# A fused attention and two-layer feed-forward kernel: where x is split, and in what order the second layer takes its blocks

## The chip, the cores and the metric

The kernel runs on one core of a Trainium2 chip. The metric is the time of one execution on the device in microseconds (us). The engines are called PE (TensorE: matmuls and transposes; its weight loads are the row PEld), DVE (VectorE), ACT (ScalarE), POOL (GpSimd) and SP (SyncE, which issues all DMAs here). Each runs its own instructions strictly in the order in which the program lists them.

## The reference

Two batches of 12 heads of softmax attention with a tanh cap, then a feed-forward layer with a softmax-weighted unit and a layer norm, then a gated feed-forward layer.

```python
scores = cap * np.tanh(scale * np.matmul(q, k.transpose(0, 1, 3, 2)) / cap)
attn = softmax(scores);  x = (attn @ v) as 896 tokens x 768          # float32
h = x @ w_in                                                          # 768 -> 1024
solu = h * softmax(h)
ln = (solu - mean(solu)) / np.sqrt(var(solu) + 1e-06) * g_ln
y = ln @ w_out                                                        # 1024 -> 768
out = (sigmoid(y @ w_gate) * (y @ w_val)) @ moe2_w_out                # 768 -> 1536 -> 768
```

The weights arrive as 64-bit floats, so the kernel receives two 32-bit words for each.

## The kernel before, in words

**Precision.** Each operand of the four big products is split in a high part (`hi`, float32 rounded to the matmul's format) and the rest (`lo`). A product is three matmuls: hi by hi, hi by lo, lo by hi (`prod`, `l1_mms`). So each weight tile and each activation tile needs a cast on ACT for hi and a subtract on DVE or POOL for lo.

**Weights.** A chunk is 128 x 512 of a weight. `chunk_steps` turns the two words of a 64-bit float into float32 and splits it, in six steps: first step (drop the sign; L349 on DVE, or L347 on ACT where `act` is set), clamp (L352), shift (L353), sign and exponent (L354), low word (L355, followed by `upper`: the scale by `g_ln`, L334, and the hi cast on ACT, L336), and the lo subtract (L339). `chunk_stream` puts the steps of many chunks into the queue `todo`, two chunks overlapping, with each chunk's DMA three chunks ahead. `fill(k)` takes the next k steps out of the queue at the place where it is called. The twelve chunks of the second layer's weight come through `w2_stream`, two for each of six output blocks; their split tiles are called `w_hl`.

**First layer and norm.** The 896 tokens go in seven tiles t of 128. `x_split(t)` makes xh (ACT, L391) and xl (L392) from x, in two buffers each. `l1_mms(t)` are 36 matmuls of 512 columns (L405) into PSUM. Then `ln_max` (DVE, L415), `ln_exp` (ACT, L420), `ln_he` (DVE, L423), `ln_stats` (DVE, L429 to L434, and a power on POOL, L435), `ln_norm` (one small DVE instruction, L439, then the pass over the tile, on ACT in L441 for tiles 2 to 6), `ln_trans` (8 transposes on PE, L449) and `ln_evac` (ACT L455 writes lnhi, DVE L456 writes lnlo). The tile `e` that L420 writes, and that the transposes read at the end, has one buffer. Tiles 0 and 1 run beside the attention. For t from 2 to 6 the loop near L590 writes out the order by hand: half of the 36 matmuls, a step of `todo`, the other half, the transposes of tile t-1, and then the norm of tile t with `fill` calls and the split for tile t+2 between its parts.

**Second layer.** `l2(m, g)` is 24 matmuls for output block m (of six) and token group g: group 0 is tiles 0 to 2 (384 columns), group 1 is tiles 3 to 6 (512 columns). It reads both `w_hl` tiles of block m, asks for four more steps of `todo` behind it, and leaves the evacuation (`y_hi` on ACT, L649, `y_lo` on DVE, L650) to run behind the next block. Its PSUM pool has two buffers.

**Order.** Until the end of the second layer PE, ACT, DVE and POOL keep the order in which the code is written (`tc.manual_schedule`). The third and fourth layers come after that; their weight chunks have the first step on ACT already.

Of the kernel before, what the change touches and what calls it, by code (L numbers as in the profile page):

```python
# [32 lines left out]
K3 = DM // P  # L33
# [109 lines left out]
def network(ctx: ExitStack, tc: tile.TileContext, sh, general, w_in, w_mid, w_gv, w_fin, outT):  # L143
    nc = tc.nc
# [159 lines left out]
    def fill(k):  # L304
        for _ in range(min(k, len(todo))):
            todo.popleft()()
# [51 lines left out]
            steps += [upper]  # L358
        return steps + [lower]

    def chunk_stream(chunks):

        raw = {}

        def load(c):
            if c < len(chunks):
                raw[c] = chunk_load(chunks[c][0])

        order = []
        for c, (src, dst, scale) in enumerate(chunks):  # L370
            steps = chunk_steps(lambda c=c: raw[c], dst, scale)
            last = steps[-1]
            steps[-1] = lambda last=last, c=c: (last(), load(c + AHEAD))
            n = len(steps)
            order += [(n // 2 * c + k + 2 * (k == n - 1), c, step) for k, step in enumerate(steps)]
        for c in range(AHEAD):
            load(c)
        todo.extend(step for _, _, step in sorted(order, key=lambda x: x[:2]))
# [34 lines left out]
    def ln_max(t):  # L413
        sts[t] = lin2.tile([P, 24], F32, tag="st", name="st")
        nc.vector.tensor_reduce(sts[t][:, 0:1], hts[t].rearrange("p a b -> p (a b)"), AX.X, ALU.max, negate=True)  # L415

    def ln_exp(t):
        st = sts[t]
        lnes[t] = lin2.tile([P, F1], F32, tag="e", name="e", bufs=1)
        nc.scalar.activation(lnes[t], hts[t].rearrange("p a b -> p (a b)"), AF.Exp, bias=st[:, 0:1], accum_out=st[:, 1:2])  # L420
# [93 lines left out]
    def w2_stream():  # L514
        chunk_stream([
            (w_mid[m].rearrange("p a b -> p (a b)")[:, c * CH:(c + 1) * CH], w2_dst(m, c), sh.g_sb[:, c * 4:c * 4 + 4])
            for m in range(K3) for c in range(2)
        ])

    NS = 2 * NPAIR  # L520
    for s in range(-1, NS):
        m = s + 1
# [45 lines left out]
    t = L1_BESIDE  # L568
# [18 lines left out]
    for t in range(L1_BESIDE, 7):  # L587
        if t == 3:
            x0.close()
        if t == 2:  # L590
            lnt2 = lns.enter_context(tc.tile_pool(name="lnt2" + sfx, bufs=1, side="right", reuse_waits="tile"))
            ln_hi[1] = lnt2.tile([P, K2, NT - G1], F32R, name="lnhi1")
            ln_lo[1] = lnt2.tile([P, K2, NT - G1], F32R, name="lnlo1")
            w2p = lns.enter_context(tc.tile_pool(name="w2p" + sfx, bufs=W2_BUFS, side="right", reuse_waits="tile"))
        k = FILL_T if wide else 0
        if t > L1_BESIDE:
            mms = l1_mms(t)
            run(mms[:18])
        fill(k)
        run(mms[18:])  # L600
        if t > L1_BESIDE:
            ln_trans(t - 1)
        else:
            run(late[:1])
        ln_max(t)
        ln_exp(t)
        if t == 6:
            ln_he(t)
            ln_stats(t)
            ln_evac(t - 1)  # L610
            ln_norm(t, True)
            fill(3 * k)
            continue
        fill(k)
        ln_he(t)
        ln_stats(t)
        if t > L1_BESIDE:
            ln_evac(t - 1)
        else:
            run(late[1:])  # L620
        if t + 2 < 7:
            x_split(t + 2, nc.gpsimd)
        fill(k)
        ln_norm(t, True)
        fill(k)
    wi.close()
    ytp = ctx.enter_context(tc.tile_pool(name="ytp" + sfx, bufs=1, side="left", reuse_waits="tile"))
    y_hi = ytp.tile([P, K3, NT], F32R, name="y_hi")
# [27 lines left out]
    l2(1, 0)  # L656
    ln_trans(6)
    ln_evac(6)
    l2(2, 0)
    for m in range(3):  # L660
        l2(m, 1)
    for m in range(3, K3):
        for g in range(2):
            l2(m, g)
    run(y_evac)
# [93 lines left out]
```

## Time and profile before

| what | value |
|---|---|
| time, median of 3 runs (lowest to highest) | 514.54 us (514.01 to 514.84) |
| time of the profiled execution | 515.4 us |
| span of its trace, first to last instruction | 513.5 us |
| PE busy over the span | 495.0 us |
| mean granted PE clock (1.0 is 2.4 GHz) | 0.993 |
| tiles 2 to 6 of the first layer and their norm | 131 to 180 us of the span |
| second layer | 180 to 251 us |
| third layer | 251 to 422 us |
| fourth layer and end | 422 to 513.5 us |

How to read it: PE is busy nearly always, so the time can fall only where PE stands idle or runs at the lower of its two clock levels, and it rises wherever PE is made to wait. The timeline view lists instructions with their start, length, and in brackets the idle time of the engine before them and what ended it.

### The profile page before, as it was taken

What the parts mean: (1) busy time and instruction counts of PE and PEld (TensorE: products, weight loads), DVE (VectorE), ACT (ScalarE), POOL (GpSimd) and SP (SyncE); (2) the same over time, 40 slices, a digit from 0 to 9 for tenths busy, and PEclk for the clock granted to TensorE, in tenths of its full rate; (3) what the DMA queues carried; (4) which work ended last, traced back from release to release, by engine and by line L of the source; (5) the groups of instructions that cost most, each with busy time, mean ns of one, the idle gap of its engine ahead of it and who ended that gap; (6) DMA issues with size and microseconds to landing.
All of it is one profiled execution on the core that took longest, in us unless ns stands there. A gap on an engine that the chain in (4) does not pass through costs nothing.

```text
span 513.5 us, 6510 instructions
## 1 busy us (share of the span) xinstructions
PE 495.0 (96%) x2480; PEld 386.8 (75%) x2480; DVE 336.4 (66%) x580; ACT 239.2 (47%) x326; POOL 57.1 (11%) x41
## 2 busy tenths in 40 slices
PE   8999999999998977999999999999999999999995
PEld 4333333553776767899899999999999999999995
DVE  1776854174788888569889888887877777551000
ACT  5999999575243432124454444434334433321000
POOL 0010101021212100000002111111111011000000
PEclk9999999999999997999999999999999999999999
DMA  7676665010101113115555444343333443500001
GB/s 253 185 214 178 207 184 157 18 38 19 61 0 41 42 43 122 58 66 165 168 160 171 141 140 123 124 123 92 106 93 122 124 123 101 158 37 37 19 36 41
DMA packets 19058, 55.04 MB, mean 107 GB/s; under 512 B 3212, under 2 KB 6156, under 8 KB 19020
## 3 DMA queue, kind: packets, MB, share of 16 engines
q1 hardware_dynamic: 19020, 54.56, 34.7%
q8 instruction: 21, 0.34, 0.3%
q14 instruction: 17, 0.14, 0.1%
HBM read 51.68 MB, written 2.79 MB: 106 GB/s over the span
## 4 chain that ended last, share of the span: by engine, by line
PE 76%; ACT 14%; DVE 7%; issue 2%; POOL 0%; ACTq 0%; POOLq 0%
PE big L635 34%; PE l4o L635 17%; PE l2o L635 11%; PE big L405 5%; ACT e L198 5%; ACT e L220 5%; PE big L192 3%; PE o L238 3%; DVE e L423 1%; ACT wi_hi L336 1%; DVE lnlo L456 1%; PE big L449 1%; PE sums L246 1%; ACT e L420 1%; PE warm L125 1%
## 5 line engine op out<-in xcount | busy, mean ns | idle before, releaser
L635 PE MATMUL big<-y_hi,w_hl 128*128 128x448 f32 x576 | 161.7, 362 | 0.0
L635 PEld LDWEIGHTS big<-y_hi,w_hl 128*128 128x128 f32 x576 | 107.9, 187 | 7.9
L635 PE MATMUL big<-y_lo,w_hl 128*128 128x448 f32 x288 | 104.6, 363 | 0.0
L336 ACT CAST w_hl<-cvt 128x512 fp32r<-128x512 f32 x66 | 40.8, 618 | 86.0 <-PE big L635 46.4
L635 PE MATMUL l4o<-p_hi,w_hl 128*128 128x448 f32 x288 | 80.7, 361 | 0.0
L355 DVE SCALAR_TENSOR_TENSOR cvt<-w_raw,cvt 128x512 uint32<-128x512 uint32 x78 | 72.8, 934 | 1.2
L635 PE MATMUL l2o<-lnhi,w_hl 128*128 128x384 f32 (+1 forms) x192 | 57.9, 379 | 6.3 <-DVE w_hl L339 6.3
L339 DVE TENSOR_TENSOR w_hl<-cvt,w_hl 128x512 fp32r<-128x512 f32 x66 | 45.3, 686 | 26.1 <-ACT w_hl L336 25.7
L347 ACT ACTIVATE cvt<-w_raw 128x512 f32<-128x512 f32 x54 | 36.2, 671 | 49.5 <-DVE w_hl L339 29.8
L635 PEld LDWEIGHTS l4o<-p_hi,w_hl 128*128 128x128 f32 x288 | 54.0, 187 | 3.9
L635 PEld LDWEIGHTS big<-y_lo,w_hl 128*128 128x128 f32 x288 | 54.1, 188 | 3.1
L354 DVE SCALAR_TENSOR_TENSOR cvt<-w_raw,cvt 128x512 uint32<-128x512 uint32 x78 | 53.6, 687 | 1.4
L708 POOL TENSOR_TENSOR p_lo<-sg,p_hi 128x896 fp32r<-128x896 f32 x12 | 30.5, 2538 | 210.7 <-ACT p_hi L707 210.7
L198 ACT ACTIVATE e<-big,cap_inv 112x896 f32<-112x896 f32 x48 | 46.6, 1038 | 14.8 <-PE big L192 14.8
L635 PE MATMUL l4o<-p_lo,w_hl 128*128 128x448 f32 x144 | 52.3, 363 | 0.0
L352 DVE TENSOR_SCALAR cvt<-cvt 128x512 f32<-128x512 f32 x78 | 33.7, 433 | 22.5 <-ACT cvt L347 22.3
L220 ACT ACTIVATE e<-e,cap_abs 112x896 f32<-112x896 f32 x48 | 48.1, 1073 | 0.0
L635 PEld LDWEIGHTS l2o<-lnhi,w_hl 128*128 128x128 f32 x192 | 37.2, 197 | 11.3 <-DVE w_hl L339 7.2
L238 PE MATMUL o<-e,v 112*64 112x448 f32 x192 | 43.4, 552 | 0.4 <-ACT to L254 0.3
L192 PE MATMUL big<-qk_raw 64*112 64x448 f32 x192 | 43.0, 559 | 0.3 <-ACT e L198 0.3
L353 DVE TENSOR_SCALAR cvt<-cvt 128x512 uint32<-128x512 uint32 x78 | 37.0, 476 | 1.6
L635 PE MATMUL l2o<-lnlo,w_hl 128*128 128x384 f32 (+1 forms) x96 | 36.0, 375 | 0.0
(81 smaller groups left out, 497.5 us busy)
## 6 DMA issues: line engine op xcount, KB each, us to landing
w_raw<-in_w_gv SPq DMA_DIRECT2D x36, 512.0 KB, 3.7
w_raw<-in_w_fin SPq DMA_DIRECT2D x18, 512.0 KB, 3.6
w_raw<-in_w_in SPq DMA_DIRECT2D x12, 512.0 KB, 4.2
w_raw<-in_w_mid SPq DMA_DIRECT2D x12, 512.0 KB, 4.9
qk_raw<-in_qk SPq DMA_DIRECT2D x12, 448.0 KB, 4.3
v<-in_v SPq DMA_DIRECT2D x12, 224.0 KB, 4.1
out_t<-ob SPq DMA_DIRECT2D x12, 224.0 KB, 2.3
qk_raw<-rd SPq DMA_DIRECT2D x22, 112.0 KB, 3.0
```

The costliest lines, as they stand in the source:

```text
L192: nc.tensor.matmul(sc[j][:KC, c, :S], r[d, 1, kc * KC:(kc + 1) * KC], r[d, 0], start=True, stop=True)
L198: nc.scalar.activation(e, es[n, u][:KC, :, :S], AF.Tanh, scale=sh.cap_inv[:KC])
L220: nc.scalar.activation(es[n, u], es[n, u], AF.Exp, scale=sh.cap_abs[:KC])
L238: nc.tensor.matmul(o[d, :S], vs[i][:, kc, d], e[j][:, c], start=(kc == 0), stop=(kc == 3))
L336: nc.scalar.copy(st["hi"], w)
L339: v.tensor_tensor(st["lo"], st["w"], f32(st["hi"]), ALU.subtract)
L347: first = lambda t, lo, hi: nc.scalar.activation(f32(t), f32(hi), AF.Abs)
L352: word(lambda t, lo, hi: v.tensor_scalar(f32(t), f32(t), as_f32(W_MOST), as_f32(W_LEAST), ALU.min, ALU.max)),
L353: word(lambda t, lo, hi: v.tensor_scalar(t, t, 3, REST, ALU.logical_shift_left, ALU.bitwise_and)),
L354: word(lambda t, lo, hi: v.scalar_tensor_tensor(t, hi, TOP, t, ALU.bitwise_and, ALU.bitwise_or)),
L355: word(lambda t, lo, hi: (v.scalar_tensor_tensor(t, lo, 29, t, ALU.logical_shift_right, ALU.bitwise_or), upper())),
L635: nc.tensor.matmul(out, l, r[kx], start=(first and m == 0), stop=(last and m == 2))
```

## The change

It does four things. In the norm loop `x_split(t + 2)` moves from behind the statistics to a place between `ln_max` and `ln_exp`, and its subtract goes from POOL to DVE. The `fill(k)` that stood between the statistics and `ln_norm` moves behind `ln_norm`. The second layer's chunks get their first step on ACT (`act=True`). And in the second layer `l2(2, 0)` no longer comes before group 1 of blocks 0 and 1; the order is now (0,0), (1,0), (0,1), (1,1), (2,0), (2,1) and so on.

```diff
-    def chunk_stream(chunks):
+    def chunk_stream(chunks, act=False):
...
-            steps = chunk_steps(lambda c=c: raw[c], dst, scale)
+            steps = chunk_steps(lambda c=c: raw[c], dst, scale, act)
...
             for m in range(K3) for c in range(2)
-        ])
+        ], act=True)
...
         ln_max(t)
+        if t + 2 < 7:
+            x_split(t + 2)
         ln_exp(t)
...
             run(late[1:])
-        if t + 2 < 7:
-            x_split(t + 2, nc.gpsimd)
-        fill(k)
         ln_norm(t, True)
-        fill(k)
+        fill(2 * k)
...
-    l2(2, 0)
-    for m in range(3):
+    for m in range(2):
         l2(m, 1)
-    for m in range(3, K3):
+    for m in range(2, K3):
         for g in range(2):
             l2(m, g)
```

The lines behind the change are numbered up to two lower than before (L650 becomes L649, L635 becomes L634).

DVE, end of the norm of tile 2 and start of that of tile 3 (`st` holds a tile's statistics, `cvt` a chunk in conversion):

```order
 L456 TENSOR_TENSOR lnlo_143<-big,lnhi_142 128x8x128
-L353 TENSOR_SCALAR cvt<-cvt 128x512
-L439 TENSOR_SCALAR st<-st 128x1
-L354 SCALAR_TENSOR_TENSOR cvt<-w_raw,cvt 128x512
-L349 TENSOR_SCALAR cvt<-w_raw 128x512
-L415 TENSOR_REDUCE st<-big 128x1
+L439 TENSOR_SCALAR st<-st 128x1
+L353 TENSOR_SCALAR cvt<-cvt 128x512
+L354 SCALAR_TENSOR_TENSOR cvt<-w_raw,cvt 128x512
+L415 TENSOR_REDUCE st<-big 128x1
+L392 TENSOR_TENSOR xl<-x_159,xh 128x768
 L339 TENSOR_TENSOR w_hl<-cvt,w_hl 128x512
```

L439 now follows lnlo directly, the step L349 is gone from DVE, and the subtract L392 stands behind the maximum L415.

ACT at the same place, tiles 2 and 3:

```order
 L336 CAST w_hl<-cvt 128x512
+L391 CAST xh<-x_159 128x768
 L420 ACTIVATE e,st<-big,st 128x1024
 L455 CAST lnhi_142<-big 128x8x128
+L441 ACTIVATE e<-e,st 128x1024
+L347 ACTIVATE cvt<-w_raw 128x512
 L391 CAST xh<-x_159 128x768
-L441 ACTIVATE e<-e,st 128x1024
 L420 ACTIVATE e,st<-big,st 128x1024
```

The cast L391 now stands ahead of the exponential L420 of its tile, and the step L347 behind the norm's last pass L441.

PE, what follows the transposes of tile 6 in the second layer, in the kernel before (`w_hl_1607` is the first weight tile of block 2, `lnhi0` and `lnlo0` are group 0):

```order
L449 MATMUL big_1612<-ident_92,e_1518 128x128 x8
L635 MATMUL l2o_1640<-lnhi0_142,w_hl_1607 128x384
L635 MATMUL l2o_1640<-lnlo0_143,w_hl_1607 128x384
L635 MATMUL l2o_1640<-lnhi0_142,w_hl_1607 128x384 x2
L635 MATMUL l2o_1640<-lnlo0_143,w_hl_1607 128x384
```

And in the changed kernel (`w_hl_1197` is the first weight tile of block 0, `lnhi1` and `lnlo1` are group 1):

```order
L449 MATMUL big_1612<-ident_92,e_1518 128x128 x8
L634 MATMUL l2o_1623<-lnhi1_1190,w_hl_1197 128x512
L634 MATMUL l2o_1623<-lnlo1_1191,w_hl_1197 128x512
L634 MATMUL l2o_1623<-lnhi1_1190,w_hl_1197 128x512 x2
L634 MATMUL l2o_1623<-lnlo1_1191,w_hl_1197 128x512
```

PE now goes on with a block whose weights it has used already, and needs the lnhi and lnlo of tile 6, just transposed, instead of the weights of block 2.

## Rows read from the trace of the kernel before

**Rows 1.** The page: busy time by engine, share of the span, instructions.

```profile
PE 495.0 (96%) x2480; PEld 386.8 (75%) x2480; DVE 336.4 (66%) x580; ACT 239.2 (47%) x326; POOL 57.1 (11%) x41
```

**Rows 2.** Timeline of PE, its six waits: start, length, instruction, [idle before, releaser].

```profile
148.92 1.09 PE L449 MATMUL big<-ident,e 128*128 128x128 f32 x8 [0.83 <-ACT e L441]
160.00 1.09 PE L449 MATMUL big<-ident,e 128*128 128x128 f32 x8 [1.79 <-ACT e L441]
169.78 1.09 PE L449 MATMUL big<-ident,e 128*128 128x128 f32 x8 [0.49 <-ACT e L441]
...
186.71 0.62 PE L635 MATMUL l2o<-lnhi,w_hl 128*128 128x384 f32 x2 [2.13 <-DVE w_hl L339]
...
190.51 0.62 PE L635 MATMUL l2o<-lnhi,w_hl 128*128 128x384 f32 x2 [1.19 <-DVE w_hl L339]
...
196.68 1.01 PE L635 MATMUL l2o<-lnhi,w_hl 128*128 128x384 f32 x2 [2.95 <-DVE w_hl L339]
```

**Rows 3.** Timeline of DVE, the conversion step behind lnlo in tiles 2 to 4.

```profile
145.80 1.67 DVE L353 TENSOR_SCALAR cvt<-cvt 128x512 uint32<-128x512 uint32 x1
...
155.49 1.94 DVE L355 SCALAR_TENSOR_TENSOR cvt<-w_raw,cvt 128x512 uint32<-128x512 uint32 x1
157.46 0.69 DVE L334 TENSOR_TENSOR cvt<-cvt,g_sb 128x512 f32<-128x512 f32 x1
...
166.57 1.75 DVE L349 TENSOR_SCALAR cvt<-w_raw 128x512 uint32<-128x512 uint32 x1
```

**Rows 4.** Timeline of POOL, the subtract of x in tile 3.

```profile
155.04 1.84 POOL L392 TENSOR_TENSOR xl<-x,xh 128x768 fp32r<-128x768 f32 x1
```

**Rows 5.** Timeline of DVE, the same steps where POOL is idle.

```profile
186.58 0.68 DVE L355 SCALAR_TENSOR_TENSOR cvt<-w_raw,cvt 128x512 uint32<-128x512 uint32 x1
...
188.36 0.43 DVE L353 TENSOR_SCALAR cvt<-cvt 128x512 uint32<-128x512 uint32 x1
...
189.43 0.42 DVE L349 TENSOR_SCALAR cvt<-w_raw 128x512 uint32<-128x512 uint32 x1
```

**Rows 6.** Timeline of ACT, the norm of tile 3.

```profile
150.10 1.12 ACT L420 ACTIVATE e<-big,st 128x1024 f32<-128x1024 f32 x1 [1.23 <-PE big L449]
...
152.10 0.84 ACT L391 CAST xh<-x 128x768 fp32r<-128x768 f32 x1
...
158.71 1.24 ACT L441 ACTIVATE e<-e,st 128x1024 f32<-128x1024 f32 x1
```

**Rows 7.** Timeline of DVE, the norm of tile 3.

```profile
151.34 1.22 DVE L423 TENSOR_TENSOR e<-big,e 128x1024 f32<-128x1024 f32 x1 [1.07 <-ACT e L420]
...
154.36 1.22 DVE L456 TENSOR_TENSOR lnlo<-big,lnhi 128x1024 fp32r<-128x1024 f32 x1
...
158.07 0.21 DVE L439 TENSOR_SCALAR st<-st 128x1 f32<-128x1 f32 x1
...
158.99 1.22 DVE L415 TENSOR_REDUCE st<-big 128x1 f32<-128x1024 f32 x1
```

**Rows 8.** Timeline of DVE, the subtract of x where DVE makes it already.

```profile
104.87 0.88 DVE L392 TENSOR_TENSOR xl<-x,xh 128x768 fp32r<-128x768 f32 x1
...
124.59 1.54 DVE L392 TENSOR_TENSOR xl<-x,xh 128x768 fp32r<-128x768 f32 x1 [1.37 <-ACT xh L391]
```

**Rows 9.** The chain that ended last: tile 6's matmuls; start, length, what.

```profile
170.87 8.23 PE big L405 x36
```

**Rows 10.** Timeline of DVE, lnlo of tile 6.

```profile
194.47 1.23 DVE L456 TENSOR_TENSOR lnlo<-big,lnhi 128x1024 fp32r<-128x1024 f32 x1 [0.70 <-ACT lnhi L455]
```

**Rows 11.** Busy time by stretch: PE, PEld, DVE, ACT, POOL (instructions), PE clock, DMA share, GB/s.

```profile
196.10:202.80 6.70, 6.12 (x19) 6.03 (x20) 6.53 (x13) 1.55 (x3) 0.00 (x0) 0.50 0.27 88
...
239.00:252.00 13.00, 13.00 (x66) 11.78 (x65) 11.95 (x23) 6.60 (x12) 0.00 (x0) 1.00 0.51 151
```

**Rows 12.** The page's groups: the first step on ACT; busy us, mean ns | idle before.

```profile
L347 ACT ACTIVATE cvt<-w_raw 128x512 f32<-128x512 f32 x54 | 36.2, 671 | 49.5 <-DVE w_hl L339 29.8
```

**Rows 13.** The waits view: us in total, times, longest.

```profile
ACT cvt L347 <- DMA w_raw<-in_w_gv: 12.0, 10, 2.4
```

## The prediction

> **What bounds the kernel now.** I read the page first: PE is busy 495.0 us of a span of 513.5 us [rows 1], so all that other engines do counts only where PE waits for it. Then the timeline of PE from 131 us on. Behind the attention PE waits six times for more than 0.3 us at places that the change touches [rows 2]. Three waits, of 0.83, 1.79 and 0.49 us, stand before the transposes of tiles 2, 3 and 4 and end with L441, the norm's last pass on ACT. Three more, of 2.13, 1.19 and 2.95 us, stand in the second layer and end with a weight's lo subtract, L339 on DVE. Together 9.4 us. Last the busy time by stretch: from 196.1 to 202.8 us the granted clock is 0.50, the lower level of 1.2 GHz, and PE's 19 matmuls there take 6.12 us [rows 11]; it fell some 2.3 us into the longest of the six waits.
>
> Why L441 comes late is read beside DVE. In tile 3 lnlo (L456) ends at 155.58, and L439, on which L441 waits, starts only at 158.07 [rows 7]: in between stand a conversion step of 1.94 us and L334 [rows 3]. The same three steps take 0.68, 0.43 and 0.42 us where POOL is idle [rows 5] and 1.94, 1.67 and 1.75 us in tiles 2 to 4 [rows 3], each while POOL makes its subtract of x, 155.04 to 156.88 in tile 3 [rows 4].
>
> **The change part by part.** *Subtract and step taken from between the statistics and L439.* L439 now follows L456. From L420's start at 150.10 to L456's end at 155.58 are 5.48 us; with L439 (0.21), L441 (1.24) and the transposes (1.09) [rows 2, 6, 7] this makes 8.0 us, some 8.2 with the handovers. This is a loop, since L420 of the next tile waits for the transposes to free `e` [rows 6]. PE itself needs 8.23 us for a tile's 36 matmuls [rows 9] and about 1 us for its transposes, 9.2 us. So the loop, which was 11.1 us in tile 3 (L420 at 150.10, transposes done at 161.09), falls below PE's own pace with about 1 us to spare, and all three waits go: 0.83 + 1.79 + 0.49 = 3.1 us. What is late next there is PE itself.
>
> *Split of x at the head of the norm.* It puts an ACT cast of 0.84 us [rows 6] ahead of L420 and a DVE subtract ahead of L423. The cast needs its buffer back from the tile's matmuls, so it starts with L415 and lies beside it (1.22 us [rows 7]): free. The subtract took 0.88 us where DVE made it undisturbed and 1.54 us beside a POOL instruction [rows 8]; I take 0.88, since POOL has none here any more. It lies in DVE's wait of 1.07 us for L420 [rows 7], beside one conversion step of some 0.4 us that stood there before; together they need about 1.2 us and have that of L420. So 0 us, at worst 3 x (1.54 - 0.88) = 2.0 us, of which the spare of 1 us per tile takes all. If that cover were gone, it would cost the 0.88 us three times.
>
> *First step on ACT.* Twelve times 0.42 us leave DVE [rows 5] and twelve times 0.67 us come to ACT [rows 12], which is busy 239 of 513 us [rows 1]. Two of them fall into the attention, behind the exponentials, where ACT then waits for PE; four stand in the norm loop behind an L441, and six between the `y_hi` of the second layer. On PE's path only one was seen on DVE, the L349 between the second layer's first wait and its second: its removal shortens the wait of 1.19 us by 0.3 to 0.4 us. I take 0.3. What queues behind an L347 on ACT is a `y_hi`, then DVE's `y_lo`, then the next L339; what holds it is the DMA of its words (a rival below). The Trainium skill's page "ScalarE: Activation LUTs" (section Rules for kernel authors) speaks against this part: simple element-wise work belongs on VectorE. The trace agrees as to the length, 671 ns on ACT [rows 12] against 0.42 us on DVE [rows 5]; if the longer step were on the path, the sum would lose 12 x 0.25 = 3 us, and by ACT's idle half it loses nothing.
>
> *The order of the second layer.* The first wait (2.13 us) stays: it hangs on the norm of tile 6 on DVE, which begins when PE has made that tile and so only moves along. The third wait was for block 2's weights. It ended at 196.68 [rows 2]. Now PE waits for lnlo of tile 6 instead, which ended at 194.47 + 1.23 = 195.70 [rows 10], 1.0 us sooner. Before, two matmuls of block 2 ran ahead of the wait; now one does, of hi by hi, so I count 0.8 us, and some 2.1 us stay idle, in two pieces. Block 2's weights get the 48 matmuls of blocks 0 and 1 in group 1 as cover, by 8.23 us for 36 of the same width [rows 9] some 11 us, and were 1 us later than lnlo.
>
> *The clock.* If it stays up, the 6.12 us of matmuls at the lower level [rows 11] take half: 3.0 us. Bounds: 0 if it falls for as long as before, 3.0 if not. I take 3.0: in the trace a wait of 2.13 us did not lower it and one of 2.95 did, and 2.1 is nearer to the first.
>
> *Sum.* 3.1 + 0.3 + 0.8 + 3.0 = 7.2 us. The profiled execution took 515.4 us (1.9 of them outside the span), so it would take 508.2; the median of the runs is 0.9 us lower, 514.54, so 507.3 us. Behind the second layer PE has the same work and no wait, and I let it move forward whole.
>
> **The rivals.** *The clock falls all the same* at one of the two stretches of 2.1 us. For: both are just as long as the wait that passed once, and it may have passed by luck of where it lay. Against: that pass. Price: 0 to 3.4 us (half of the 6.7 us at the lower level); less at the first stretch, where the slower matmuls fill the wait behind them. About 2.6 us in the middle: 509.9 us. The Trainium skill's "TensorE: Matmul & The Clock Gate" (HAM oscillation) says that pauses between groups of matmuls bring the clock down, and this change leaves pauses; the wait of 2.95 us agrees, the five shorter ones do not.
>
> *The norm's waits do not close.* If the cast and the subtract of x are not covered, each loop grows by 0.84 + 0.88 = 1.7 us to 9.9 us, longer than PE's 9.2, and with a stretched subtract to 10.6: three waits of 0.7 to 1.4 us come back, 2 to 4 us. 510.4 us. Against: PE's end starts both, and the hole before L423 is there.
>
> *The third layer's weights come late.* PE reaches that layer 7 us sooner, while DVE is busy 11.95 of 13.0 us around the turn [rows 11], and the third layer's first chunks are loaded behind the second's. An L347 that waits for its DMA (ten such waits, 2.4 us at the longest [rows 13]) now stands ahead of the last `y_hi`. One or two full waits reach PE: 2.4 to 4.8 us back, 511 us. Against: DVE is rid of some steps, and walking the new order with the old durations I find the weights there 1 us or more before PE (an estimate).
>
> *Slower than before: ACT held by DMA through the whole second layer.* Six L347 stand there, each ahead of a `y_hi`. If all wait the longest that an L347 waited, 2.4 us [rows 13], and 0.9 us of each is covered, 6 x 1.5 = 9.0 us come back where 7.2 were won: 516.3 us. It decides from 1.2 us that pass uncovered on the mean. Against: the words are ordered three chunks ahead, and the waits view has no wait of DVE for the second layer's words.
>
> **How the numbers follow.** The forecast, 507.3 us with its own range of 506.4 to 508.3, has 0.50; the fallen clock 0.30; the norm's waits 0.07; the third layer 0.08; slower 0.03. The last 0.02 I leave to no change at all (the median of before), since the waits might be set by something that the trace names wrongly. The range of 506.3 to 511.0 leaves out the worst of the clock's case together with another, and the last two. What a measurement of this kernel can tell from no change is about 0.2%, 1.0 us; the chances: faster 0.94, within it 0.03, slower 0.03.
>
> **What would show it.** In the trace of the changed kernel: no wait of PE before the transposes of tiles 2 to 5; L439 right behind L456 and the conversion steps at 0.4 to 0.7 us throughout; L392 on DVE at about 0.9 us ahead of L423; a first wait in the second layer of still 2.1 us, the second of about 0.8, then two short ones on lnhi and lnlo; no stretch at clock 0.50 until the end; PE without a wait from there to the fourth layer. Wrong would be: a wait of PE on L441 as before, L423 waiting for L392, a wait of PE on `y_lo` or on L339 behind the second layer's first three blocks, or the clock down again.

## The result and the profile after

The changed kernel took 508.96 us (median; 508.72 to 509.00), the kernel before 514.54 us. The ratio is 0.989, with a 95% interval of 0.9875 to 0.9906. The forecast was 507.3 us with a range of 506.3 to 511.0: direction and range hold, the point is 1.7 us too low. The profiled execution took 508.99 us with a span of 507.2 us.

The page of the changed kernel, which answers to [rows 1]: busy time by engine, share of the span, instructions.

```profile
PE 493.2 (97%) x2480; PEld 385.4 (76%) x2480; DVE 332.5 (66%) x571; ACT 245.6 (48%) x338; POOL 50.0 (10%) x38
```

DVE has nine instructions fewer: twelve first steps went to ACT and three subtracts came from POOL, as the three on POOL less show.

The timeline of PE in the changed kernel: every wait of more than 0.3 us behind 140 us, against the six of [rows 2]. Columns: start, length, instruction, [idle before, releaser].

```profile
182.68 0.62 PE L634 MATMUL l2o<-lnhi,w_hl 128*128 128x384 f32 x2 [2.15 <-DVE w_hl L339]
...
186.13 0.62 PE L634 MATMUL l2o<-lnhi,w_hl 128*128 128x384 f32 x2 [0.85 <-DVE w_hl L339]
...
190.11 0.49 PE L634 MATMUL l2o<-lnhi,w_hl 128*128 128x512 f32 x1 [1.10 <-ACT lnhi L455]
...
191.37 0.50 PE L634 MATMUL l2o<-lnlo,w_hl 128*128 128x512 f32 x1 [0.77 <-DVE lnlo L456]
```

The three waits for L441 are gone. The first wait in the second layer is as long as before, the second went from 1.19 to 0.85, and in place of the 2.95 stand 1.10 and 0.77.

The timeline of DVE in tile 3 of the changed kernel, against [rows 3] and [rows 7]:

```profile
149.05 0.95 DVE L392 TENSOR_TENSOR xl<-x,xh 128x768 fp32r<-128x768 f32 x1
149.91 0.68 DVE L339 TENSOR_TENSOR w_hl<-cvt,w_hl 128x512 fp32r<-128x512 f32 x1
150.52 1.22 DVE L423 TENSOR_TENSOR e<-big,e 128x1024 f32<-128x1024 f32 x1
...
153.53 1.22 DVE L456 TENSOR_TENSOR lnlo<-big,lnhi 128x1024 fp32r<-128x1024 f32 x1
154.67 0.20 DVE L439 TENSOR_SCALAR st<-st 128x1 f32<-128x1 f32 x1
154.79 0.68 DVE L355 SCALAR_TENSOR_TENSOR cvt<-w_raw,cvt 128x512 uint32<-128x512 uint32 x1
```

L439 follows lnlo directly, the step L355 takes 0.68 us where it took 1.94, and L392 takes 0.95 us ahead of L423.

Busy time by stretch in the changed kernel, against [rows 11]: PE, PEld, DVE, ACT, POOL (instructions), PE clock, DMA share, GB/s.

```profile
192.10:195.60 3.50, 3.50 (x11) 2.69 (x10) 1.91 (x4) 0.62 (x1) 0.00 (x0) 0.51 0.38 117
```

So the clock fell here too: PE's records show the lower level from 192.12 to 195.53, 3.41 us, and it fell 0.75 us behind the last of the four waits. Before it fell at 196.06 for 6.83 us.

**The time by stretch.** A run's span also holds the start of the kernel, where the granted clock rises from its lower level at 4.06 to 7.20 us, differently in each profile here, and moves all that follows by up to 1.5 us (half of the 3.14 us between the two is 1.57). To take that out I measure from one instruction that all kernels share, PE's L296 near 134 us, to the first matmul of the second layer (the norm loop), from there to the first of the third layer behind the last of the second, and from there to the end of the span. Of the changed kernel these are the rows at 134.07, 175.68 and 244.54:

```profile
134.07 0.60 PE L296 MATMUL big<-ident,rw 112*128 112x112 f32 x4 [0.73 <-DVE rw L292]
...
175.68 0.42 PE L634 MATMUL l2o<-lnhi,w_hl 128*128 128x384 f32 x1
...
244.54 0.36 PE L634 MATMUL big<-y_lo,w_hl 128*128 128x448 f32 x1
```

| kernel | median us | L296 at | norm loop | second layer | rest | from L296 | lower clock at, for us |
|---|---|---|---|---|---|---|---|
| before (profiled run 515.4) | 514.54 | 134.30 | 45.44 | 71.50 | 262.26 | 379.20 | 196.06, 6.83 |
| changed | 508.96 | 134.07 | 41.61 | 68.86 | 262.66 | 373.13 | 192.12, 3.41 |
| e1_order_only | 513.13 | 134.48 | 45.43 | 69.38 | 262.41 | 377.22 | 196.51, 3.41 |
| e2_norm_only | 510.80 | 134.28 | 41.62 | 70.43 | 262.27 | 374.32 | 182.90, 3.41 and 193.14, 3.41 |
| e3_fill_only | 512.66 | 134.74 | 43.71 | 70.17 | 262.28 | 376.16 | none |
| e4_split_only | 512.12 | 133.87 | 42.85 | 72.42 | 262.26 | 377.53 | 184.97, 6.83 and 195.21, 3.41 |
| e5_no_act | 509.35 | 133.96 | 41.62 | 69.41 | 262.51 | 373.54 | 192.14, 3.41 |
| e6_dummy_pe | 508.18 | 134.83 | 41.64 | 67.43 | 262.70 | 371.77 | 183.60, 3.41 |
| e7_trans_mid (profiled 506.28) | 504.33 | 134.80 | 41.61 | 65.36 | 262.73 | 369.70 | 183.91, 3.41 |
| e8_trans_mid_fill | 505.89 | 134.88 | 41.62 | 66.21 | 262.69 | 370.52 | 190.57, 3.41 |
| e9_pool_head | 509.85 | 135.13 | 42.03 | 67.45 | 262.59 | 372.07 | 184.14, 3.41 |
| e10_mid_first | 504.74 | 135.39 | 41.61 | 63.86 | 262.74 | 368.21 | none |
| e11_dummy_all | 508.18 | 134.62 | 41.62 | 67.25 | 262.61 | 371.48 | none |
| e12_evac_early | 503.68 | 135.16 | 41.64 | 62.69 | 262.71 | 367.04 | none |

The last column leaves out the lower level at the start and at the end of each span. The span is read to 0.1 us, so "rest" and "from L296" are good to 0.05. The border between "second layer" and "rest" is not the same in all kernels: some matmuls of the third layer, 0.20 us each, already run ahead of the last of the second. They are 12 in the kernel before (from 239.12 on), e2, e3 and e4, 11 in e1 and e5, and 10 in the changed kernel (from 234.96 on) and the others. So the change gained 3.83 us in the norm loop and 2.64 us less those two matmuls, 2.2 us, in the second layer; the 0.40 by which the rest seems to grow are the same two matmuls. Together these are 6.07 us. The spans differ by 6.3, since in these two runs L296 also stands 0.23 us apart.

### The profile page after: what moved, and what is told of

It is laid out like the page before. It is cut to its first block, busy times and chain, and to the rows that moved or that the text cites. A ratio compares the mean times of both kernels' runs of the same rounds, so it can differ in the third digit from the quotient of the medians.

```text
span 507.2 us, 6531 instructions
## 1 busy us (share of the span) xinstructions
PE 493.2 (97%) x2480; PEld 385.4 (76%) x2480; DVE 332.5 (66%) x571; ACT 245.6 (48%) x338; POOL 50.0 (10%) x38
## 3 DMA queue, kind: packets, MB, share of 16 engines
q1 hardware_dynamic: 19020, 54.56, 35.0%
## 4 chain that ended last, share of the span: by engine, by line
PE 82%; ACT 13%; DVE 3%; issue 1%; POOL 0%; ACTq 0%; POOLq 0%
PE big L634 34%; PE l4o L634 17%; PE l2o L634 11%; PE big L405 10%; ACT e L198 5%; ACT e L220 5%; PE big L192 3%; PE o L238 3%; ACT wi_hi L336 1%; PE big L449 1%; PE sums L246 1%; PE warm L125 1%; ACT to L254 1%; DVE st L415 0%; DVE e L423 0%
## 5 line engine op out<-in xcount | busy, mean ns | idle before, releaser
L634 PE MATMUL big<-y_hi,w_hl 128*128 128x448 f32 x576 | 161.8, 362 | 0.0
L634 PEld LDWEIGHTS big<-y_hi,w_hl 128*128 128x128 f32 x576 | 107.9, 187 | 8.0
L634 PE MATMUL big<-y_lo,w_hl 128*128 128x448 f32 x288 | 104.6, 363 | 0.0
L634 PE MATMUL l4o<-p_hi,w_hl 128*128 128x448 f32 x288 | 80.7, 361 | 0.0
L336 ACT CAST w_hl<-cvt 128x512 fp32r<-128x512 f32 x66 | 40.7, 617 | 68.2 <-PE big L634 41.8
L355 DVE SCALAR_TENSOR_TENSOR cvt<-w_raw,cvt 128x512 uint32<-128x512 uint32 x78 | 71.5, 919 | 1.3
L347 ACT ACTIVATE cvt<-w_raw 128x512 f32<-128x512 f32 x66 | 44.2, 670 | 55.9 <-DVE w_hl L339 34.4
L339 DVE TENSOR_TENSOR w_hl<-cvt,w_hl 128x512 fp32r<-128x512 f32 x66 | 47.1, 714 | 25.1 <-ACT w_hl L336 24.8
L634 PE MATMUL l2o<-lnhi,w_hl 128*128 128x384 f32 (+1 forms) x192 | 56.5, 373 | 4.1 <-DVE w_hl L339 3.0
L634 PEld LDWEIGHTS l4o<-p_hi,w_hl 128*128 128x128 f32 x288 | 54.0, 187 | 3.9
L634 PEld LDWEIGHTS big<-y_lo,w_hl 128*128 128x128 f32 x288 | 54.1, 188 | 3.0
L634 PE MATMUL l4o<-p_lo,w_hl 128*128 128x448 f32 x144 | 52.3, 363 | 0.0
L352 DVE TENSOR_SCALAR cvt<-cvt 128x512 f32<-128x512 f32 x78 | 32.7, 419 | 20.8 <-ACT cvt L347 20.8
L634 PEld LDWEIGHTS l2o<-lnhi,w_hl 128*128 128x128 f32 x192 | 36.2, 192 | 9.3 <-DVE w_hl L339 3.6
L634 PE MATMUL l2o<-lnlo,w_hl 128*128 128x384 f32 (+1 forms) x96 | 35.7, 372 | 0.8 <-DVE lnlo L456 0.8
L192 PEld LDWEIGHTS big<-qk_raw 64*112 64x112 f32 x192 | 15.6, 172 | 26.4 <-issue 19.3
```

What stands on the lines that cost most here:

```text
L192: nc.tensor.matmul(sc[j][:KC, c, :S], r[d, 1, kc * KC:(kc + 1) * KC], r[d, 0], start=True, stop=True)
L336: nc.scalar.copy(st["hi"], w)
L339: v.tensor_tensor(st["lo"], st["w"], f32(st["hi"]), ALU.subtract)
L347: first = lambda t, lo, hi: nc.scalar.activation(f32(t), f32(hi), AF.Abs)
L352: word(lambda t, lo, hi: v.tensor_scalar(f32(t), f32(t), as_f32(W_MOST), as_f32(W_LEAST), ALU.min, ALU.max)),
L355: word(lambda t, lo, hi: (v.scalar_tensor_tensor(t, lo, 29, t, ALU.logical_shift_right, ALU.bitwise_or), upper())),
```

## The experiments

The kernel before took 514.88, 514.76, 514.56 and 515.17 us (medians of 9 or 10 runs) beside the four groups of runs. Ratios are against these.

**e1_order_only**: the kernel before with the new order of the second layer alone.

```diff
-    l2(2, 0)
-    for m in range(3):
+    for m in range(2):
         l2(m, 1)
-    for m in range(3, K3):
+    for m in range(2, K3):
```

> The kernel before with the second layer's new order alone. Theory (the order saves by its shorter wait and by the clock): PE's waits in the norm stay at 0.83, 1.79 and 0.49 us, the second layer's at 2.1 and 1.2 us; the third, 2.95 us on a weight, becomes two on lnhi and lnlo of 2.1 us together, and the lower clock level lasts 3.4 us or less where it lasted 6.8. Gain 2.0 to 3.5 us. Rival (the order only moves the wait): gain under 0.8 us, the lower clock as long as before.

Measured: 513.13 us, ratio 0.9964 (0.9952 to 0.9976). The medians differ by 1.75 us, the profiled runs from L296 on by 1.98, nearly all of it in the second layer (71.50 to 69.38, of which 0.2 is the border). By the medians that is just below the lower end of the theory: the order gains, and the clock fell for 3.41 us, as the theory allowed. In its timeline of PE the waits of 1.10 and 0.76 us stand where the 2.95 stood.

**e2_norm_only**: the kernel before with the split at the head and the `fill` behind `ln_norm`, without `act` and with the old order (the diff of the change less its first two and last three lines).

> The kernel before with the two edits in the norm loop alone: split of x at the head with its subtract on DVE, and the conversion steps behind L439. Theory: the three waits before the transposes go, 3.1 us; the second layer keeps its waits of 2.1, 1.2 and 2.9 us and its stretch at the lower clock. Gain 2.8 to 3.3 us. Rival (cast and subtract come onto the loop): waits of 0.7 to 1.4 us stay per tile, gain under 1.5 us.

Measured: 510.80 us, ratio 0.9920 (0.9906 to 0.9934): 4.1 us, more than expected. From L296 on the profiled runs differ by 4.9: 3.82 us in the norm loop and 1.07 in the second layer, whose code is as before. The timeline of PE in the second layer has two waits left of the three of [rows 2]:

```profile
182.89 1.01 PE L634 MATMUL l2o<-lnhi,w_hl 128*128 128x384 f32 x2 [2.15 <-DVE w_hl L339]
...
192.86 0.79 PE L634 MATMUL l2o<-lnhi,w_hl 128*128 128x384 f32 x2 [2.95 <-DVE w_hl L339]
```

The stretches at the lower clock, of 3.41 us each, lie behind these two:

```profile
182.90:186.30 3.40, 3.40 (x11) 3.40 (x12) 3.30 (x7) 1.62 (x3) 0.00 (x0) 0.50 0.45 154
193.10:196.60 3.50, 3.50 (x12) 3.25 (x11) 3.40 (x8) 1.00 (x2) 0.00 (x0) 0.51 0.45 150
```

The first of them lies where PE, in the kernel before, next waited for L339, for 1.19 us. The slow matmuls take that time instead, and the wait is gone. So the same 6.8 us at the lower clock cost less here than in the kernel before, and the second layer's part of this gain belongs to where the clock fell.

**e3_fill_only** and **e4_split_only**: each half of the norm's change alone. In e3 the split stays on POOL behind the statistics and only the `fill` moves; in e4 the split goes to DVE at the head and the `fill` stays.

```diff
 # e3
             x_split(t + 2, nc.gpsimd)
-        fill(k)
         ln_norm(t, True)
-        fill(k)
+        fill(2 * k)
 # e4
         ln_max(t)
+        if t + 2 < 7:
+            x_split(t + 2)
         ln_exp(t)
...
-        if t + 2 < 7:
-            x_split(t + 2, nc.gpsimd)
```

> The kernel before with one edit: the conversion step between the statistics and L439 moves behind L439; the subtract of x stays on POOL in its old place. Theory A (what delayed L439 is any step queued ahead of it): the three waits go all the same, gain 2.8 to 3.3 us, though the step behind L439 is still stretched to 1.7 to 1.9 us by POOL's subtract. Theory B (the delay is POOL's subtract itself, which slows whatever DVE does then): little changes, gain under 1 us.

> The kernel before with the other edit of the norm loop: the split of x at its head with the subtract on DVE; the conversion step stays between lnlo and L439. Theory A (the step's place delays L439): steps take their 0.4 to 0.7 us, the waits of tiles 2 and 4 close, tile 3 keeps some 1.2 us since its step is L355 with L334 and the cast behind it; gain 1.5 to 2.2 us. Theory B (only POOL's subtract delayed it): all three waits go, 3.1 us.

Measured: e3 512.66 us, ratio 0.9956 (0.9942 to 0.9969); e4 512.12 us, ratio 0.9945 (0.9931 to 0.9959). The norm loop, which the two theories speak of, shortened by 1.73 us in e3 and by 2.59 in e4. Neither alone gives the 3.83 of both. By the medians e3 gained 2.2 and e4 2.8 us, each between its two theories; e4's profiled run is its longest, with two falls of the clock in the second layer and a mean clock of 0.988 where the other four have 0.995 to 0.997. In e4 one wait is left, in tile 3, before the transposes:

```profile
157.73 1.09 PE L449 MATMUL big<-ident,e 128*128 128x128 f32 x8 [1.01 <-ACT e L441]
```

There L355 and L334 stand between lnlo and L439, at their plain lengths of 0.68 and 0.69 us, as the theory said. In e3 two waits are left, of 0.62 and 1.00 us, which I had not walked. The timeline of DVE in e3 tells why, in tile 3:

```profile
155.65 0.20 DVE L439 TENSOR_SCALAR st<-st 128x1 f32<-128x1 f32 x1
155.77 1.82 DVE L355 SCALAR_TENSOR_TENSOR cvt<-w_raw,cvt 128x512 uint32<-128x512 uint32 x1
157.63 0.69 DVE L334 TENSOR_TENSOR cvt<-cvt,g_sb 128x512 f32<-128x512 f32 x1
158.24 0.42 DVE L352 TENSOR_SCALAR cvt<-cvt 128x512 f32<-128x512 f32 x1
158.69 0.43 DVE L353 TENSOR_SCALAR cvt<-cvt 128x512 uint32<-128x512 uint32 x1
159.04 1.22 DVE L415 TENSOR_REDUCE st<-big 128x1 f32<-128x1024 f32 x1
```

L439 is on time, but the steps that went behind it now run without a gap up to the next tile's maximum L415, and one of them is still stretched to 1.82 us by POOL. From L415 of tile 3 (148.91) to that of tile 4 are 10.1 us, more than PE's 9.2: DVE itself had become the loop. Taking the work from between lnlo and L439 helps only if it finds room elsewhere, and the removal of the stretch makes that room.

The second layer of e3 has the code of the kernel before, and in its profiled run the clock stayed up. There PE waits four times, not three. The last two waits, in block 2:

```profile
195.14 0.62 PE L634 MATMUL l2o<-lnhi,w_hl 128*128 128x384 f32 x2 [2.95 <-DVE w_hl L339]
...
198.93 0.62 PE L634 MATMUL l2o<-lnhi,w_hl 128*128 128x384 f32 x2 [1.19 <-DVE w_hl L339]
```

The fourth does not show in the kernel before, because the matmuls at the lower clock take that time. From the end of the third wait to the third layer are 53.48 us in e3 and 54.56 in the kernel before. So the 6.83 us at the lower clock cost 1.1 us there, not half of 6.12.

**e5_no_act**: the changed kernel without `act=True`.

> The changed kernel without its third part: the second layer's first conversion steps stay on DVE (L349). Theory: only the L349 ahead of the second weight of block 1 lies on PE's path; the second layer's second wait is 1.2 us and not 0.85, and the time is 0.3 to 0.4 us above the changed kernel. Rival (moving twelve steps off DVE is what carries the gain): over 1.5 us slower.

Measured: 509.35 us, ratio 0.9894 (0.9879 to 0.9910): 0.4 us above the changed kernel, by the medians and from L296 on. The second wait is 1.19 us again, the others are as with `act`, and the clock falls at the same place for as long. This term of the sum was right, 0.3 to 0.4.

**e6_dummy_pe**: the changed kernel with dummy transposes, whose results are not used, in the two last waits of the second layer (8 before block 0 of group 1, 6 behind its first matmul).

```diff
+        if m == 0 and spins:
+            spin(spins)
...
+    spin(8)
     for m in range(2):
-        l2(m, 1)
+        l2(m, 1, 0 if m else 6)
```

> The changed kernel with idle PE time filled: 8 transposes that nobody reads between the transposes of tile 6 and the first matmul of group 1, 6 more behind that matmul. The waits on lnhi and lnlo keep their ends; only PE is busy meanwhile. Theory (the clock falls because of these two pauses, and costs half of its 3.4 us): no stretch at the lower level before the end, 1.4 to 1.8 us faster than the changed kernel. Rival (the fall has another cause, or costs nothing since the work has slack): the same time within 0.5 us.

Measured: 508.18 us, ratio 0.9867 (0.9852 to 0.9882), 0.8 us less than the changed kernel by the medians and 1.4 from L296 on. The size is near the theory, the reason is not: the clock fell once more, at 183.60, right behind the wait of 2.15 us, which it had passed in the profile of the changed kernel. It lay over the place of the 0.85 us wait, and the slow matmuls filled that.

**e11_dummy_all**: dummy transposes in all four waits (those of e6 and these).

```diff
+        for c in range(head):
+            nc.tensor.transpose(o[:, c % 4 * P:(c % 4 + 1) * P], ident, ident)
         for kk in range(K2):
+            if kk == 4 and mid:
+                spin(mid)
...
-    l2(1, 0)
+    l2(1, 0, head=15, mid=6)
```

> The changed kernel with dummy transposes (their results are overwritten) in all four waits of PE in the second layer: 15 before block 1, 6 in its middle, 8 before block 0 of group 1 and 6 behind its first matmul. They shorten no wait; they only keep PE at work in it. It tells whether the 1.7 us by which the changed kernel missed the forecast is the lower clock behind those waits. Theory: the clock stays at 2.4 GHz from its first rise to the end of the second layer in every run, and the time is 507.0 to 507.7 us (508.96 less half of 3.41 us). Rival: the clock falls for another reason than PE's pauses: it falls again, and the time stays at 508.2 us or more, as with dummy work in the last two waits alone.

Measured: 508.18 us (507.27 to 508.68), ratio 0.9875 (0.9860 to 0.9890). In the profiled run the clock stays up, and the waits that remain are 0.51, 0.43 and 0.23 us:

```profile
182.00:200.00 18.00, 16.74 (x92) 14.11 (x91) 13.52 (x25) 7.19 (x11) 0.03 (x1) 1.00 0.28 89
```

Its second layer is 67.25 us, 1.61 less than the changed kernel's, against half of 3.41 = 1.7 expected. The median is not at the 507.0 to 507.7 of the theory, though: it is 0.8 us below the changed kernel's, not 1.6, and the same as e6's, whose clock fell at another place. Of the difference 0.55 us lies ahead of L296 in the profiled run (134.62 against 134.07), where the clock rose at 5.45 instead of 4.38 us; for the other runs only the mean clocks are there, 0.997 to 0.999 against 0.995 to 0.996. So by stretch, one profile against one, the fallen clock cost 1.6 us at its place in the changed kernel; the medians show half of that.

**e9_pool_head**: the changed kernel with the subtract of x on POOL at the new place.

```diff
-            x_split(t + 2)
+            x_split(t + 2, nc.gpsimd)
```

> The changed kernel with the subtract of x (L392) back on POOL, at its new place at the head of the norm. Question: is it POOL's subtract that stretches the DVE steps beside it, wherever it stands? Theory: yes. The one DVE step that lies beside it in each of tiles 2 to 4 (L352 in tile 2, L339 in tile 3, L354 in tile 4) takes about 1.7 to 2.0 us in place of 0.42 to 0.69 us, as it did behind the statistics before, so L423 starts about 0.5 us later than in the changed kernel, where L392 takes 0.95 us of the same hole. The loop of a tile was 8.2 us and PE's own pace is 9.2, so the time stays within 0.4 us of the changed kernel (508.96). Rival: the steps were long for another reason (their place behind lnlo); then they take 0.4 to 0.7 us here and L423 never waits.

Measured: 509.85 us, ratio 0.9911 (0.9896 to 0.9926), 0.9 us above the changed kernel where at most 0.4 was expected; the norm loop is 0.42 longer (42.03 against 41.61), and the rest of the 0.9 is not explained by the one profile. Timeline of POOL and of DVE in tiles 2 to 4 of this kernel:

```profile
140.69 1.84 POOL L392 TENSOR_TENSOR xl<-x,xh 128x768 fp32r<-128x768 f32 x1 [4.63 <-ACT xh L391]
...
149.71 1.85 POOL L392 TENSOR_TENSOR xl<-x,xh 128x768 fp32r<-128x768 f32 x1 [3.25 <-ACT xh L391]
...
159.22 1.85 POOL L392 TENSOR_TENSOR xl<-x,xh 128x768 fp32r<-128x768 f32 x1 [3.46 <-ACT xh L391]
```

```profile
141.05 1.77 DVE L352 TENSOR_SCALAR cvt<-cvt 128x512 f32<-128x512 f32 x1
142.74 1.21 DVE L423 TENSOR_TENSOR e<-big,e 128x1024 f32<-128x1024 f32 x1
...
150.11 2.00 DVE L339 TENSOR_TENSOR w_hl<-cvt,w_hl 128x512 fp32r<-128x512 f32 x1
...
159.56 2.07 DVE L354 SCALAR_TENSOR_TENSOR cvt<-w_raw,cvt 128x512 uint32<-128x512 uint32 x1
```

Three other steps than in [rows 3], at another place, and each is long only there: 1.77, 2.00 and 2.07 us against 0.42, 0.68 and 0.69. The rival (the place behind lnlo made them long) is out. Each ends 0.3 to 0.6 us behind POOL's subtract (142.82 behind 142.53, 152.11 behind 151.56, 161.63 behind 161.07), which is its own length less 0.13 us in all three, as for a step that waits for POOL and then runs. The Trainium skill's page "SBUF — State Buffer" (section SBUF: two separate sides) says so: when a GpSimd instruction meets a VectorE instruction that has two SBUF inputs or runs in a mode that uses both ports, the one that started first holds their shared pair of ports to its end, and the other blocks. These rows agree; L352 has one input, and no row shows in which mode it ran.

This profile also bears on the clock. PE's waits in the second layer of e9:

```profile
184.16 1.01 PE L634 MATMUL l2o<-lnhi,w_hl 128*128 128x384 f32 x2 [2.16 <-DVE w_hl L339]
...
191.78 0.49 PE L634 MATMUL l2o<-lnhi,w_hl 128*128 128x512 f32 x1 [1.10 <-ACT lnhi L455]
...
193.04 0.50 PE L634 MATMUL l2o<-lnlo,w_hl 128*128 128x512 f32 x1 [0.76 <-DVE lnlo L456]
```

The clock fell at 184.14, by the first of them as in e6, and the slow matmuls covered the wait of 0.85; behind 1.10 and 0.76 it stayed up. The second layer took 67.45 us, 1.4 less than the changed kernel's, without any dummy work. So the place of the fall alone can account for e6's gain, and its dummy transposes need not be the reason.

**e7_trans_mid**: the changed kernel with the transposes of tile 6 in the middle of block 1 of group 0, where PE has other work while lnhi and lnlo are made.

```diff
-    l2(1, 0)
-    ln_trans(6)
-    ln_evac(6)
+    l2(1, 0, 4, lambda: (ln_trans(6), run(y_evac), ln_evac(6)))
```

> The changed kernel with the transposes of tile 6 in the middle of l2(1, 0), between its two weights, and the evacuation of l2(0, 0) and lnhi, lnlo of tile 6 behind them. Theory: the transposes fill PE's wait of 0.85 us for the second weight, lnlo is done some 1.5 us sooner and its wait lies under the block's second half; the wait of 1.9 us in two pieces shrinks to 0.3 us or less and the clock stays up: 3.5 to 4.5 us faster than the changed kernel. Rival (DVE is the bound there: what leaves the one wait comes back as another): under 1.5 us faster.

Measured: 504.33 us (503.87 to 506.28), ratio 0.9798 (0.9783 to 0.9814), 4.6 us below the changed kernel, where 3.5 to 4.5 were expected. Only the first wait, 2.15 us, is left. The profiled run, the longest of the five, has the clock down behind it for 3.41 us; the other runs' mean clocks are 0.996 to 0.998 against its 0.993, so in some of them it seems to have stayed up longer; no trace shows it.

**e8_trans_mid_fill**: e7 with one conversion step more in the norms of tiles 5 and 6, to have block 1's first weight earlier.

> As the kernel with the transposes in the middle, with one conversion step more in the norm of tile 5 and one in that of tile 6, in DVE's waits for L420 (1.02 and 1.35 us). Theory: the first weight of block 1 is ready before PE wants it, the wait of 2.15 us goes, and some 1 us of it comes back before lnlo of tile 6; 0.7 to 1.5 us faster than the kernel with the transposes in the middle. Rival (DVE's steps of tile 6 only move from behind the norm to ahead of it and make L423 late): no faster.

Measured: 505.89 us, ratio 0.9825 (0.9810 to 0.9839), slower than e7 by 1.6 us where 0.7 to 1.5 us faster was expected (0.8 by the profiled runs from L296 on; the runs of each spread over more than 2 us). The wait of 2.15 us is gone, and PE waits for other things:

```profile
184.18 1.09 PE L449 MATMUL big<-ident,e 128*128 128x128 f32 x8 [1.07 <-ACT e L441]
188.30 0.49 PE L635 MATMUL l2o<-lnhi,w_hl 128*128 128x512 f32 x1 [0.93 <-ACT lnhi L455]
189.56 0.50 PE L635 MATMUL l2o<-lnlo,w_hl 128*128 128x512 f32 x1 [0.77 <-DVE lnlo L456]
```

The timeline of ACT shows what held lnhi:

```profile
186.33 0.62 ACT L336 CAST w_hl<-cvt 128x512 fp32r<-128x512 f32 x1 [1.63 <-DVE cvt L334]
186.86 0.47 ACT L651 CAST y_hi<-l2o 128x384 fp32r<-128x384 f32 x1
187.23 1.02 ACT L455 CAST lnhi<-big 128x1024 fp32r<-128x1024 f32 x1
```

The transposes were done near 185.3, but lnhi stands behind the cast L336, and that waits for L334 on DVE, one of the four steps that follow block 0. The wait was not for the work but for its place in the queue.

**e10_mid_first**: e8 with those four steps moved behind the evacuation of tile 6, and the extra step of tile 5 moved behind the first 18 matmuls of tile 6, so that two things differ (the expectation speaks of tile 6's extra step; it is tile 5's that moved). Against e8:

```diff
-        fill(k)
+        fill(2 * k if t == 6 else k)
...
-        fill(2 * k if t == 5 else k)
+        fill(k)
...
-    l2(0, 0)
-    l2(1, 0, 4, lambda: (ln_trans(6), run(y_evac), ln_evac(6)))
+    l2(0, 0, more=0)
+    l2(1, 0, 4, lambda: (ln_trans(6), run(y_evac), ln_evac(6), fill(FILL_2 if wide else 0)))
```

> The kernel that had the transposes of tile 6 in the middle of block 1 and one more conversion step in the norms of tiles 5 and 6, with the four conversion steps that followed block 0 moved behind the evacuation of tile 6 (so that y_hi, lnhi and lnlo queue behind no cast that waits for DVE), and the extra step of tile 6 moved behind its first 18 matmuls. Walked with the measured lengths: PE waits about 0.7 us for L441 before the transposes, then less than 0.3 us in all until block 1 of group 1; the weights of block 1 and 2 are in time. The wait of 2.15 us is gone. Theory (conversion steps ahead of the evacuation were what made the previous trial slow): 502.3 to 503.2 us, against 504.3 of the kernel with the transposes in the middle alone, and with no pause over 1 us the clock stays at 2.4 GHz from its first rise to the end of the second layer. Rival: something else holds lnhi and lnlo, or the weights of block 2 come late: 504.5 us or more.

Measured: 504.74 us, ratio 0.9809 (0.9796 to 0.9822), 1.2 us less than e8, but above the 502.3 to 503.2 of the theory and no better than e7's 504.33. lnhi follows the transposes and its two waits are gone, the clock stays up, but a wait appears that I had not walked:

```profile
194.53 0.50 PE L635 MATMUL l2o<-lnhi,w_hl 128*128 128x512 f32 x1 [0.89 <-DVE y_lo L652]
```

The `y_lo` of block 1 waits for its `y_hi`, which on ACT stands behind two casts L336 that wait for DVE: eight conversion steps come first now. The PSUM pool has two buffers, so PE waits for the evacuation.

**e12_evac_early**: e10 with that evacuation directly behind block 1.

```diff
-    l2(1, 0, 4, lambda: (ln_trans(6), run(y_evac), ln_evac(6), fill(FILL_2 if wide else 0)))
+    l2(1, 0, 4, lambda: (ln_trans(6), run(y_evac), ln_evac(6), fill(FILL_2 if wide else 0)), more=0)
+    run(y_evac)
+    fill(FILL_2 if wide else 0)
```

> The kernel of the previous trial (transposes of tile 6 in the middle of block 1, evacuation of tile 6 ahead of the conversion steps) with one more move: the evacuation of block 1 (y_hi, y_lo of group 0) directly behind that block and ahead of the next four conversion steps, since in that trial PE waited 0.89 us for this y_lo, which stood behind eight steps. Theory: that wait goes, nothing else changes, and one pause of about 1.06 us is left in the second layer: 0.9 us less than 504.74, that is 503.6 to 504.1 us, with the clock up to the end of the second layer. Rival: the weights of block 2, whose last steps now stand behind the y_lo, come late in its place: 504.5 us or more.

Measured: 503.68 us (503.43 to 504.11), ratio 0.9781 (0.9767 to 0.9794), as expected. One wait of 1.07 us is left in the second layer, and the clock stays up; all five runs have a mean clock of 0.999 or 1.0. This version is faster than both kernels, by 5.3 us than the changed one.

## Why the prediction was right, and where it was off

**What bounds, and which waits go: right.** PE's waits came out as walked: none before the transposes, 2.15 us in the second layer as before, 0.85 for "about 0.8", and two short ones on lnhi and lnlo of 1.9 us together for "some 2.1". e3, e4 and e9 show the cause: both the steps ahead of L439 and POOL's subtract beside them had to go, and the steps are long wherever that subtract runs. At the head of the norm it does little harm even on POOL: e9 keeps all but 0.42 of the 3.83 us.

**The norm's three waits: the term was 3.1 us and measured 3.83.** I summed the idle times of [rows 2]. A wait costs PE more than its idle. Last matmuls before the transposes of tile 2 in the kernel before:

```profile
147.70 0.39 PE L405 MATMUL big<-wi_hi,xl 128*128 128x512 f32 x1
148.92 1.09 PE L449 MATMUL big<-ident,e 128*128 128x128 f32 x8 [0.83 <-ACT e L441]
149.77 0.48 PE L405 MATMUL big<-wi_hi,xh 128*128 128x512 f32 x1
```

And in the changed kernel:

```profile
147.47 0.40 PE L405 MATMUL big<-wi_hi,xl 128*128 128x512 f32 x1
147.71 1.04 PE L449 MATMUL big<-ident,e 128*128 128x128 f32 x8
148.50 0.48 PE L405 MATMUL big<-wi_hi,xh 128*128 128x512 f32 x1
```

From L405 to the next L405 are 2.07 us there and 1.03 here: the wait of 0.83 cost 1.04 us. In tiles 3 and 4 the same stretch is 3.03 and 1.73 us, so the waits of 1.79 and 0.49 cost 2.00 and 0.70. Matmuls overlap, one starting 0.23 us behind another though each lasts 0.39, and a wait loses that overlap. Three times 0.2 us are most of the missing 0.7.

**The second layer: 0.3 + 0.8 for the waits and 3.0 for the clock forecast, 2.2 measured in all.** The idle fell from 6.27 to 4.87 us, and one wait more costs 0.2; that gives 1.2 for the waits and leaves 1.0 for the clock. But the 6.27 hide a wait under the slow matmuls. Against the 7.29 us that e3 idles with the clock up, the waits are worth about 2.4, and the clock's part is negative: 1.1 for the fall that went, less 1.6 for the one that came. The sum of the two is measured; how it divides depends on which is taken out first.

**The clock: the term was 3.0 us. This step failed, in two ways.** The first is that the clock fell again. "In the trace a wait of 2.13 us did not lower it and one of 2.95 did, and 2.1 is nearer to the first" took one pass for a rule. It fell for 3.41 us behind the waits of 1.10 and 0.77, and e11 puts the price at 1.6 us. That is the rival that the clock falls all the same, with its 0.30, at the second of its two places and for 1.6 instead of 2.6 us (the middle of its own bounds of 0 and 3.4 is 1.7, which gives 509.0). The second is the price: by e3 the stretch at the lower clock cost the kernel before 1.1 us and not half of 6.12, since block 2's second weight was late too. With the clock up the change would have gained 3.8 us in the second layer (71.50 to e11's 67.25, less 0.4 for the border), near the forecast 4.1. That is luck: the new order takes away the hidden wait, which the sum did not know.

What makes the clock fall is open. It fell in e7, whose only wait there is one of 2.15 us, and it passed that very wait in the changed kernel; it stayed up in e3 with waits of 1.96, 1.19, 2.95 and 1.19 us, though two of e3's five runs have a mean clock of 0.992 against 0.997 in the profiled one. It fell in e8 with three waits of 1.07, 0.93 and 0.77 us close together, and stayed up in e10 with 1.06 and 0.89, in e12 with 1.07 alone and in e11, where dummy work stood in the waits. It fell behind 1.10 and 0.77 in the changed kernel and passed them in e9. So no length of a single wait in these traces decides it. That less idle time keeps the clock up is what e10 to e12 suggest; what decides in the cases between is open.

**The base: 0.9 us too much.** I took the 7.2 us from the profiled execution of the kernel before, 515.4, and then took off another 0.9 for the median. But that run was longer than the median for the same 6.83 us at the lower clock that the sum had removed. Of 37 runs of the kernel before beside the experiments, 24 with a mean granted clock of 0.992 or 0.993 have a median of 515.1 us and 13 with 0.994 or 0.995 one of 514.3. The changed kernel's runs all lie within 0.3 us, and its profiled run at their median. So most of the 0.9 was counted twice; this is argued from the mean clocks, since these runs left no trace.

**The rest.** That PE moves forward whole behind the second layer was right: the 0.40 us of the table are the border, two matmuls of 0.20, and e1 and e5, which differ from the kernel before by one, show 0.15 and 0.25. The sum then reads 3.83 + 2.2 = 6.0 from L296 on, and the 0.23 us ahead of it come with the run's start. The point is only 1.7 us low because errors cancelled in part: the second layer's 1.9 and most of the base's 0.9 were too much, the norm's 0.7 and the start's 0.2 too little. That is luck too. The rivals on the third layer's weights, on the norm's waits and on ACT held by its DMA did not come true: PE has no wait over 0.3 us behind 191.37.

## What to carry to other kernels

A step that waits behind a queue is late by everything that stands ahead of it on its engine: against e8, e10 and e12 got most of their time not by less work but by letting the short instruction that PE waits for go first. Count a wait of PE from start to start against an unhindered pair, not by its idle, and compare kernels from an instruction that they share. Where the clock falls in the run that the sum is made against, take it out of both the sum and the base, or of neither, and price it as a chance rather than as a term. Before halving the time of slow matmuls, ask which wait would stand in their place.

## What the runs showed of the hardware

- A DVE step beside POOL's subtract of 1.84 us took 1.56 to 2.07 us in place of 0.42 to 0.69, whichever step it was and wherever it stood. lnlo, which reads PSUM, took its usual 1.22 us although POOL's subtract began within it [rows 4, 7].
- Between its first rise and the end of the second layer the clock was down for 3.41 or 6.83 us at a time in every profile here that shows it down. The price depends on what lies under it: 1.6 us for 3.41 where PE had work throughout (changed kernel against e11), 0.2 where the slow matmuls covered a wait of 0.85 (e6 and e9, 67.43 and 67.45 against 67.25), and 1.1 for 6.83 where they covered one of 1.19 (kernel before against e3).
- The clock's first rise came between 4.06 and 7.20 us from the start of the span, and with it L296 moved from 133.87 to 135.39: though nearly the same work stands ahead of it, a difference as large as some of the effects measured here.
